# Laying out the backward step's results by SBUF-to-SBUF transfers in place of TensorE transposes in three blocks of four (S4 convolution with a gated FFN, one Trainium2 core)

## The chip, the core and the metric

The kernel runs on one core of one Trainium2 chip. The metric is the device time of one execution in microseconds (us). A core has TensorE (PE; its weight loads are listed apart as PEld), VectorE (DVE), ScalarE (ACT), GpSimd (POOL) and SyncE (SP), which here only issues DMA transfers. Transfers can be issued from SyncE's, ScalarE's and GpSimd's queues. Each engine works through its own instructions in order; semaphores tie the engines together.

## The reference

```python
x  = A_u                                    # (1, 2048, 512)
xn = layernorm(x)
s  = A_ref(xn, ...)                         # S4 convolution along the 2048 steps
g  = silu(gelu(xn @ w1 + b1) @ w2 + b2)     # F = 1792
return x + s * g

# A_ref, for each of D = 512 channels, N = 128 states:
P = exp((dt * A)[:, :, None] * arange(L))   # complex
K = einsum("dn,dnl,dn->dl", C, P, dt * B).real
y = irfft(rfft(u, 2L) * rfft(K, 2L))[:L] + u * Dskip
```

All arrays are float32. The change lies in the convolution: the product of two spectra and the way back from it.

## The kernel before

The first part (until about 404 us of the span) computes the layer norm, the feed-forward network and the 512 convolution kernels. Its order is written out by hand in `ORDER`, token by token. It ends with the gate `g` in DRAM (`gd`) and the kernels in DRAM (`kgd`). The change doesn't touch it.

The second part does the convolution in `NB = 4` blocks of 128 channels. The transform of 2048 points is split as 32 x 64. For each block `b` there are eight steps `g`, and `slot(b, g)` (L1020) writes down what each step issues. `tc.manual_schedule()` keeps that order on every engine. The functions, in the order of a step:

- `second_dft(b, g)` (L874): 64 small matmuls into a PSUM tile "ri" of two buffers; L883 in the profile.
- `last_dft(b - 1, t)` (L969, matmuls L975) of the block before: the last, 32-point transform of the way back. It reads `yy[b, q4, "s"]` and the table `gc`, and writes two banks. In blocks 1 and 2 it runs in steps 5 and 7; for block 2, within block 3, in step 4 and at the very end.
- `last_out` (L978) multiplies its result with the gate on VectorE (L982, into `gb`) and adds `x` on GpSimd (L983, into `xb`); `store` (L985) sends `xb` out by eight transfers on SyncE's queue (L992).
- `first_dft(b + 1, ...)` (L856, matmuls L864) in even steps: the first transform of the next block; `first_out` (L867) copies it to `X` on ScalarE (L870).
- `back_dft(b, j, h)` (L914, matmuls L918) in odd steps, for the group `j` whose products were made two steps earlier; four matmuls for each half `h`, each 128x128. Step 1 does group 3 of the block before.
- `spectrum` (L887) copies half of the spectrum to `uh` on ScalarE (L891).
- `back_out(b, j, h)` (L921) copies the result of `back_dft` from PSUM into the tile `Z` on ScalarE (L930).
- `product` (L896) on VectorE (L900), and in odd steps `combine` (L902), four instructions on VectorE (L912, L910) that make the tile `Y`, the operand of `back_dft`.
- `swings(b - 1, q4)` (L997): `swing` (L932) turns four 128x128 pieces of `Z` by TensorE transposes (L936), `swing_out` (L939) copies them from PSUM to an SBUF tile "bs" (L944). For blocks 0 and 1 these run in steps 3 and 5 of the next block, two `q4` in each; for block 2 in steps 2 to 5 of block 3, one in each; for block 3 at the end.
- `tail_load` (L949): loads `gb` (from `gd`, L961 or L955) and `xb` (from the input, L964 or L957) for the later `last_out`. A tail is six transfers on SyncE's queue. The tiles have three buffers, so the load of the fourth tail of a block (step 5) follows the stores of step 5 in the queue. In block 3, GpSimd's queue carries the tails of block 3 (steps 1 to 4) beside SyncE's for block 2 (steps 0 to 3).
- `side_load`, `side_turn`, `kernel_load`, `side_skip`: inputs for the block after the next one, in steps 3, 6 and 7 of blocks 0 and 1.

PSUM tiles from `bank` (L804) go round over four banks in turn. After the 32 steps, the rest of block 3 is written out by hand (L1125 to L1144).

In the profiled execution the second part starts at 405.9 us. Block 1 starts (its first `second_dft`) at 436.5, block 2 at 473.1, block 3 at 509.6.

Of the kernel before, what the change touches and what calls it, by code (L numbers as in the profile page):

```python
# [11 lines left out]
F32 = mybir.dt.float32  # L12
# [8 lines left out]
P = 128  # L21
# [4 lines left out]
N1, N2 = 32, 64  # L26
NB = 4
# [25 lines left out]
G.4 S.1.3 W.6 S.2.0 WS.4.3.1 S.2.1 R.3 A.0.0 H.4 KL.1.0 LC.3 TF.2.0 S.2.2 S.2.3 TH.2.0 B.0.0 WS.5.0  # L53
TF.3.0 WS.5.1 C.0.0 TH.3.0 WB.6 BB TL.2.0 A.0.1 WS.5.2 KL.0.1 Z.0 S.3.0 TL.3.0 B.0.1 TF.3.1 TH.3.1 C.0.1
TL.3.1 WS.5.3.1 P.1 LD.2 P.0 LD.3 WS.6.0 S.3.1 WS.6.1 S.3.2 S.3.3 A.1.0 LS.5.1 TF.2.1 N.0.0 TH.2.1 F.5.0
LS.4.1 B.1.0.1 F.5.1 KL.1.1 WS.6.2 TL.2.1 N.0.1 G.5 C.1.0 R.4 F.6.0 LK.0 S.4.0 S.4.1 A.1.1 KL.2.0 F.6.1
B.1.1 LR.4 E.0.0 H.5 F.7.0 G.6 Z.1 F.7.1 WS.6.3 C.1.1 H.6 A.2.0 F.8.0 S.4.2 E.0.1 E.0.2 KL.2.1 R.5 N.1.0
N.1.1 B.2.0.1 Q.0 R.6 G.7 Z.2 LC.4 C.2.0 E.1.0 E.1.1 KL.3.0 F.8.1 S.4.3 U.0 H.7 S.5.0 G.8 S.5.1 A.2.1
B.2.1 KL.3.1 P.1 LD.4 F.9.0 C.2.1 TF.4.0 KL.4.0 UD.0 R.7 LC.5 F.9.1 E.1.2 S.5.2 P.1 N.2.0 G.9 TH.4.0
S.5.3 A.3.0 TF.4.1 LL.6 S.6.0 Q.1 S.6.1 H.8 B.3.0.1 C.3.0 S.6.2 S.6.3 TL.4.0 A.3.1 KL.4.1 N.2.1 O.0.0 U.1  # L60
B.3.1 LD.5 O.0.2 O.0.1 E.2.0 F.10.0 P.1 Z.3 TH.4.1 UD.1 C.3.1 S.7.0 S.7.1 KL.5.0 N.3.0 E.2.1 TL.4.1
F.10.1 E.2.2 N.3.1 P.1 O.0.3 S.7.2 A.4.0 R.8 E.3.0 B.4.0.1 H.9 F.11.0 S.7.3 G.10 C.4.0 S.8.0 LS.6.0 Q.2
# [68 lines left out]
def _shape_constants():  # L131
    n1 = np.arange(N1)[:, None]
    k1 = np.arange(N1)[None, :]
    a = 2 * np.pi * n1 * (k1 + 0.25) / N1
    cf = np.tile(np.stack([np.cos(a), -np.sin(a)], 1), (G, 1, 1))
    cg = np.zeros((2, N1, 2, 3, N1))
    for hh in range(2):
        for c, v in enumerate((np.cos(a).T, -np.sin(a).T)):
            cg[hh, :, c, 0] = v
            cg[hh, :, c, 1:].reshape(N1, N1, 2)[:, :, hh] = v  # L140
    cg = cg.reshape(P, 3 * N1)
    n2 = np.arange(N2)[:, None]
    k2 = np.arange(N2)[None, :]
    cm = np.zeros((2, N2, N1, 3, N2))
    ct = np.zeros((2, N2, N1, 2, N2))
    for k in range(N1):
        th = 2 * np.pi * (n2 * (k + 0.25) / L + n2 * k2 / N2)
        c, s = np.cos(th), np.sin(th)
        cm[:, :, k, 0, :] = c
        cm[:, :, k, 1, :] = s  # L150
        cm[:, :, k, 2, :] = -s
        ct[0, :, k, 0, :] = c.T / L
        ct[1, :, k, 0, :] = -s.T / L
        ct[0, :, k, 1, :] = s.T / L
        ct[1, :, k, 1, :] = c.T / L
    ct = ct.reshape(P, N1, 2, 2, 2, 16).transpose(0, 1, 4, 5, 3, 2)
    cb = np.zeros((CH, NPC, CH, NPH))
    for d in range(CH):
        cb[d, :3, d, :N1] = N2 * np.arange(N1)
        cb[d, :3, d, N1:] = np.arange(N2 // 2) + 0.5  # L160
        cb[d, 3:, d, :N1] = 1.0
    f = np.float32
    return {
        "cf": cf.reshape(P, 2 * N1).astype(f),
        "cg": cg.astype(f),
        "cm": cm.reshape(P, N1 * 3 * N2).astype(f),
        "ct": ct.reshape(P, N1 * P).astype(f),
        "cb": cb.reshape(CH * NPC, CH * NPH).astype(ml_dtypes.bfloat16),
    }
# [3 lines left out]
def kernel(  # L173
# [5 lines left out]
    V, A, GP, PE, SY = nc.vector, nc.scalar, nc.gpsimd, nc.tensor, nc.sync  # L179
# [121 lines left out]
    SB = {}  # L301
# [4 lines left out]
    sg = ExitStack()  # L306
# [544 lines left out]
    def side_skip(b):  # L851
        for h in range(2):
            k0 = side[b][1][h][:, :, 0]
            GP.tensor_add(k0, k0, dsk[:, b, h * DB // 2:(h + 1) * DB // 2])
# [17 lines left out]
    sp, sm, yy = {}, {}, {}  # L872
# [41 lines left out]
    def back_dft(b, j, h):  # L914
        Y = yy[b, j].rearrange("p j a m -> p (j a) m")
        p = bank(f"sa{b}_{j}_{h}")
        for e in range(4):
            PE.matmul(p[:, e, :], Y[:, 4 * h + e, :], SB["tcn"][:, 8 * j + 4 * h + e, :], start=True, stop=True)  # L918
        yy[b, j, h] = p

    def back_out(b, j, h, engs=(A,)):  # L921
        if (b, "Z") not in yy:
            yy[b, "Z"] = SB["pm"].tile([P, 32, 2, N1, 2], F32, tag="Z", name=f"Z{b}", bufs=2)
        k = 8 * j + 4 * h
        src = yy.pop((b, j, h)).rearrange("p k (x h c) -> p x h k c", h=2, c=2)
        dst = yy[b, "Z"][:, :, :, k:k + 4, :]
        w = 4 // len(engs)
        for i, eng in enumerate(engs):
            n = slice(w * i, w * i + w)
            eng.copy(dst[:, :, :, n], src[:, :, :, n]) if eng is A else eng.tensor_copy(dst[:, :, :, n], src[:, :, :, n])  # L930

    def swing(b, q4, jj, wide=None):  # L932
        Z = yy[b, "Z"].rearrange("p (j r t q) h k c -> p j r t q (h k c)", j=2, r=2, t=2)
        p = bank(f"w{b}_{q4}_{jj}") if wide is None else wide[:, jj]
        for e in range(4):
            PE.transpose(p[:, e, :], Z[:, jj, q4 // 2, q4 % 2, e, :], ident)  # L936
        yy[b, q4, jj] = p
# [28 lines left out]
    def new_tail(b, q4):  # L966
        return tuple(SB["pm"].tile([P, 4, P], F32, tag=m, name=f"{m}{b}_{q4}", bufs=3) for m in ("gb", "xb"))
# [29 lines left out]
    def swings(b, q4, wide=None, engs=(A, A)):  # L997
        for jj in range(2):
            swing(b, q4, jj, wide)
            if wide is None:  # L1000
                swing_out(b, q4, jj, engs[jj])
        if wide is not None:
            for jj in range(2):
                swing_out(b, q4, jj, engs[jj])
# [15 lines left out]
    def slot(b, g):  # L1020
        nxt = b + 1 < NB
        i = g // 2
        sa = (b, i - 1) if i else (b - 1, 3)
        if sa[0] < 0 or g % 2 == 0:
            sa = None
        last = b == NB - 1
        sw = {2: (0,), 3: (1,), 4: (2,), 5: (3,)} if last else {3: (0, 1), 5: (2, 3)}
        ls = {4: (0,)} if last else {5: (0,), 7: (1,)}
        second_dft(b, g)
        if b:  # L1030
            for q4 in ls.get(g, ()):
                last_dft(b - 1, q4)
                if not last:
                    last_out(b - 1, q4, (GP, GP))
                    store(b - 1, q4)
        if nxt and g % 2 == 0:
            first_dft(b + 1, i // 2, i % 2, range(G))
        if sa:
            back_dft(*sa, 0)
            back_dft(*sa, 1)  # L1040
        spectrum(b, g)
        if nxt and g % 2 == 0:
            first_out(b + 1, i // 2, i % 2)
        if sa:
            back_out(*sa, 0)
            back_out(*sa, 1)
        product(b, g)
        if (b, g) == (0, 0):
            gx[0, 0, "t"] = new_tail(0, 0)
        if g % 2 and (b, g) != (NB - 1, 7):  # L1050
            combine(b, i, 1, V)
        if b == NB - 1 and g > 5:
            js = slice(2 * g - 12, 2 * g - 10)
            combine(b, 3, 1, V, js)
            combine(b, 3, 0, V, js)
        elif g % 2:
            combine(b, i, 0, V)
        if last:
            for q4 in ls.get(g, ()):
                last_out(b - 1, q4, (GP, GP))  # L1060
                store(b - 1, q4)
        if b:
            for q4 in sw.get(g, ()):
                swings(b - 1, q4)
        if last and g == 0:
            big = SB["pf"].tile([P, 2, N1, P], F32, tag="X0", name="last")
            for q4 in range(4):
                gx[b, q4, "t"] = (big[:, 0, 4 * q4:4 * q4 + 4], big[:, 1, 4 * q4:4 * q4 + 4])
        if last and g == 2:
            spare = SB["pf"].tile([P, 4, 4, P], F32, tag="in", name="spare", bufs=2)  # L1070
            for i in range(2):
                gx[b - 1, 2 + i, "t"] = (spare[:, 2 * i], spare[:, 2 * i + 1])
        when = (0, 1, 2, 3) if last else (0, 1, 2, 5)
        if b and g in when:
            tail_load(b - 1, when.index(g))
        if last and 0 < g < 5:
            tail_load(b, g - 1, GP, g > 2)
        if last and g == 0:
            SY.dma_start(gc2, cg[:, N1:])
        if b + 2 < NB and g == 3:  # L1080
            side_load(b + 2)
        if b + 2 < NB and g == 6:
            side_turn(b + 2)
            kernel_load(b + 2)
        if b + 2 < NB and g == 7:
            side_skip(b + 2)

    with tc.manual_schedule():
        prologue()
# [5 lines left out]
    with tc.manual_schedule():  # L1095
# [9 lines left out]
        for p in "S0 F00 S1 S2 F01 S3 L0 F10 L1 A0 F11 A1 L2 L3 A2 A3".split():  # L1105
            if p[0] == "F":
                k = int(p[1]), int(p[2])
# [17 lines left out]
        b = NB - 1  # L1125
# [49 lines left out]
```

## Time and profile before

| | |
|---|---|
| median of 3 runs | 559.72 us (559.51 to 559.85) |
| profiled execution | 559.77 us, its span 558.0 us |
| granted TensorE clock, mean | 0.998 |
| instructions | 17143 |
| DMA traffic | 86.92 MB in 108345 packets |
| busy in 418 to 434 us (block 0), of 16.0 | PE 16.00, DVE 12.14, ACT 9.13, POOL 1.04 |
| busy in 480 to 498 us (block 2), of 18.0 | PE 18.00, DVE 10.97, ACT 10.84, POOL 0.00 |
| busy in 514 to 528 us (block 3), of 14.0 | PE 13.66, DVE 12.30, ACT 6.40, POOL 6.46 |

How to read the lines of the profile. In a timeline a line is: start (us from the span's start), length (us), engine, line of the kernel, operation, written tile <- read tiles, shapes, how many in a row (x), and in square brackets how long the engine stood idle before it and what it then waited for. Lines of one kind that follow one another are merged, so the length of "x16" is that of all sixteen together; matmuls overlap, so the distance to the next line's start says what they cost. "SPq", "ACTq" and "POOLq" are the issuing of transfers; the transfer itself goes on afterwards. In a group line the fields are: line, engine, operation, tiles, shapes, count | busy us, mean ns of one | idle us before. A line of DMA issues gives written tile <- read tensor, queue, count, KB each, and the median time from issue to landing.

### The profile page before, as it was taken

To read this page: it belongs to the slowest core of one execution; us is meant where nothing else is said; L and a number is where in the kernel's file an instruction comes from. 1 tells how busy PE (TensorE), PEld (TensorE's weight loads), DVE (VectorE), ACT (ScalarE), POOL (GpSimd) and SP (SyncE) were. 2 spreads that over 40 slices of the span, in tenths; PEclk is the share of its full clock that TensorE was granted. 3 is DMA by queue.
4 is the path that set the end of the run, shared out by engine and by line. 5 is a ranking of instruction groups with operands and counts; after the bars stand their busy time and mean duration, and the time that the engine had idled before them with its cause. 6 is when DMAs were issued, how large, how long until landed. Compare 5 with 4: busy or idle time off the path is not lost.

```text
span 558.0 us, 17143 instructions
## 1 busy us (share of the span) xinstructions
PE 540.2 (97%) x7179; PEld 432.1 (77%) x7179; DVE 454.2 (81%) x697; ACT 407.8 (73%) x602; POOL 296.3 (53%) x403
## 2 busy tenths in 40 slices
PE   8899999999999999999999999999999999999995
PEld 7567777777777777767777777777889998988872
DVE  6899999999997799988988969877357657767874
ACT  3589997977598999668989798995355565564542
POOL 5639585776966769857718747540320305014323
PEclk9999999999999999999999999999999999999999
DMA  8959337267468392426167049205965583615945
GB/s 188 288 161 311 84 96 210 61 210 228 135 189 269 133 295 81 143 75 192 57 188 219 21 114 186 61 11 181 365 245 79 140 128 95 191 46 127 197 120 113
DMA packets 108345, 86.92 MB, mean 156 GB/s; under 512 B 44294, under 2 KB 87562, under 8 KB 108268
## 3 DMA queue, kind: packets, MB, share of 16 engines
q1 hardware_dynamic: 97584, 65.37, 43.8%
q0 software_dynamic: 9568, 19.93, 12.1%
q8 instruction: 56, 0.92, 0.7%
q10 hardware_dynamic: 1116, 0.53, 0.4%
q14 instruction: 21, 0.17, 0.1%
HBM read 52.25 MB, written 33.55 MB: 154 GB/s over the span
## 4 chain that ended last, share of the span: by engine, by line
PE 68%; DVE 16%; issue 6%; DMA 5%; SPq 2%; ACT 1%; POOL 1%; DVEq 0%; POOLq 0%
PE z L295 8%; PE z L296 7%; PE z L297 7%; PE f L256 7%; PE f L258 7%; PE f L257 7%; PE s L883 6%; PE kg L656 5%; PE s L864 4%; PE sa L918 3%; DMA w2s<-in_B_w_dram 2%; PE ph L595 2%; PE w L936 2%; DVE e L641 2%; DVE hl L282 2%
## 5 line engine op out<-in xcount | busy, mean ns | idle before, releaser
L618 POOL TENSOR_TENSOR mm<-mm,rc 128x32 f32<-128x32 f32 (+4 forms) x150 | 110.7, 738 | 11.8
L295 PE MATMUL z<-w2h,hh 128*128 128x512 f32 x224 | 97.9, 437 | 0.0
L256 PE MATMUL f<-xh,w1h 128*128 128x512 f32 x220 | 92.0, 418 | 0.5 <-ACT hf L270 0.5
L297 PE MATMUL z<-w2h,hl 128*128 128x512 f32 x224 | 88.5, 395 | 0.9 <-DVE hl L282 0.9
L296 PE MATMUL z<-w2l,hh 128*128 128x512 f32 x224 | 88.7, 396 | 0.0
L258 PE MATMUL f<-xh,w1l 128*128 128x512 f32 x220 | 86.9, 395 | 1.5 <-DVE w1l L241 1.5
L257 PE MATMUL f<-xl,w1h 128*128 128x512 f32 x220 | 86.7, 394 | 0.0
L883 PE MATMUL s<-X,mc 64*64 64x128 f32 x2048 | 63.5, 272 | 0.9 <-issue 0.9
L900 DVE TENSOR_TENSOR t<-s,uh 128x512 f32<-128x512 f32 x64 | 41.1, 685 | 25.9 <-ACT uh L891 25.6
L883 PEld LDWEIGHTS s<-X,mc 64*64 64x64 f32 x2048 | 56.0, 133 | 4.8 <-issue 2.7
L641 DVE TENSOR_TENSOR e<-mm,ra 128x1024 f32<-128x1024 f32 x32 | 47.8, 1495 | 4.7 <-POOL mm L618 3.2
L297 PEld LDWEIGHTS z<-w2h,hl 128*128 128x128 f32 x224 | 42.1, 188 | 11.7 <-DVE hl L282 1.8
L258 PEld LDWEIGHTS f<-xh,w1l 128*128 128x128 f32 x220 | 41.3, 188 | 11.9 <-DVE w1l L241 2.1
L615 POOL COPY mm<-rc 128x32 f32<-128x32 f32 x30 | 15.4, 512 | 65.4 <-DVE e L648 49.0
L256 PEld LDWEIGHTS f<-xh,w1h 128*128 128x128 f32 x220 | 41.5, 189 | 10.3 <-ACT hf L270 1.2
L282 DVE TENSOR_TENSOR hl<-hf,hh 128x512 fp32r<-128x512 f32 x56 | 46.7, 838 | 3.4 <-ACT hh L276 3.3
L295 PEld LDWEIGHTS z<-w2h,hh 128*128 128x128 f32 x224 | 42.5, 190 | 9.0
L609 DVE SCALAR_TENSOR_TENSOR ra<-ra,ph 128x512 f32<-128x512 f32 x64 | 43.6, 681 | 6.9 <-ACT ra L603 6.0
L296 PEld LDWEIGHTS z<-w2l,hh 128*128 128x128 f32 x224 | 42.3, 189 | 7.9
L257 PEld LDWEIGHTS f<-xl,w1h 128*128 128x128 f32 x220 | 41.4, 188 | 8.9
L870 ACT COPY X<-s 128x512 f32<-128x512 f32 x56 | 28.9, 598 | 25.6 <-PE s L864 25.6
L645 DVE TENSOR_TENSOR e<-mm,ra 128x1024 f32<-128x1024 f32 x32 | 45.6, 1425 | 0.0
(185 smaller groups left out, 1146.2 us busy)
## 6 DMA issues: line engine op xcount, KB each, us to landing
x<-in_A_u_dram SPq DMA_DIRECT2D x16, 256.0 KB
xs<-x SPq DMA_DIRECT2D x16, 256.0 KB
xt_h<-xh POOLq DMA_DIRECT2D x4, 1024.0 KB, 5.4
xt_l<-xl POOLq DMA_DIRECT2D x4, 1024.0 KB, 7.3
kgd<-ko SPq DMA_DIRECT2D x32, 128.0 KB
za<-zo SPq DMA_DIRECT2D x4, 1024.0 KB
xh<-xt_h POOLq DMA_DIRECT2D x4, 1024.0 KB, 6.8
xl<-xt_l POOLq DMA_DIRECT2D x4, 1024.0 KB, 10.1
```

The costliest lines, as they stand in the source:

```text
L256: PE.matmul(p, wh[:, k, :], xh[:, k, :], start=(k == 0), stop=False)
L257: PE.matmul(p, wh[:, k, :], xl[:, k, :], start=False, stop=False)
L258: PE.matmul(p, wl[:, k, :], xh[:, k, :], start=False, stop=(k == KD - 1))
L282: V.tensor_sub(hl, hf, hh)
L295: PE.matmul(z, hh[:, s], wh, start=(f0 == 0 and not rows), stop=False)
L296: PE.matmul(z, hh[:, s], wl, start=False, stop=False)
L297: PE.matmul(z, hl[:, s], wh, start=False, stop=(f0 == FA - 1))
L609: V.scalar_tensor_tensor(ra[:, 0, c], ra[:, 1, c], MAGIC, p, op0=ALU.subtract, op1=ALU.subtract)
L618: GP.tensor_mul(mv[:, :, 0:3:2, w:2 * w], mv[:, :, 0:3:2, 0:w], rc[:, 2 + 2 * i:4 + 2 * i, :].rearrange("p j c -> p c j").unsqueeze(3).to_ ...
L641: V.tensor_mul(e1, m1.unsqueeze(1).to_broadcast([P, 2, CH, N1]), ra[:, :, :, :N1])
L645: V.tensor_mul(e2[:, :, :, :H], m2[:, :, :H].unsqueeze(1).to_broadcast([P, 2, CH, H]), ra[:, :, :, dn])
L883: PE.matmul(p[ka * 64:(ka + 1) * 64, r, o, :, jj], mc[h, k, ((0, 2), (1, 0))[c][o], :], xf[b][h, c, :, k, :], start=(c == 0), stop=(c == 1 ...
```

## The change

In blocks 0, 1 and 2 the transposes are left out. `back_dft` swaps its two operands there, so that its result already has the channels along the row (`p` holds, for each `k`, 128 positions by 128 channels). `spread_out` copies that from PSUM to an SBUF tile `v` on ScalarE, in place of `back_out`. `spread` then issues four transfers from SBUF to SBUF. Each takes one `k`: 128 partitions with 512 bytes each go to four partitions of the tile `S` (`8 j + k`, and 32, 64 and 96 further), 16 KB to each. There are eight spreads to a block, one at the end of a step, alternately from ScalarE's queue (odd steps) and GpSimd's (even steps), from step 3 of the block to step 2 of the next: 96 transfers in all, 64 KB each. After the last of them `S` is taken as the operand of `last_dft`. Block 3 goes on as before, with the order of rows in `Z` and in the tables `cg` and `ct` changed to fit both forms.

```diff
-    cg = np.zeros((2, N1, 2, 3, N1))
+    cg = np.zeros((2, 2, N1, 3, N1))
     for hh in range(2):
         for c, v in enumerate((np.cos(a).T, -np.sin(a).T)):
-            cg[hh, :, c, 0] = v
-            cg[hh, :, c, 1:].reshape(N1, N1, 2)[:, :, hh] = v
+            cg[hh, c, :, 0] = v
+            cg[hh, c, :, 1:].reshape(N1, N1, 2)[:, :, hh] = v
...
-    ct = ct.reshape(P, N1, 2, 2, 2, 16).transpose(0, 1, 4, 5, 3, 2)
+    ct = ct.reshape(P, N1, 2, 2, 2, 16).transpose(0, 1, 3, 2, 4, 5)
...
         for e in range(4):
-            PE.matmul(p[:, e, :], Y[:, 4 * h + e, :], SB["tcn"][:, 8 * j + 4 * h + e, :], start=True, stop=True)
+            w, m = SB["tcn"][:, 8 * j + 4 * h + e, :], Y[:, 4 * h + e, :]
+            PE.matmul(p[:, e, :], *((w, m) if b < NB - 1 else (m, w)), start=True, stop=True)
         yy[b, j, h] = p
+
+    def spread_out(b, j, h):
+        if h == 0:
+            yy[b, j, "v"] = SB["pm"].tile([P, 8, P], F32, tag="bs", name=f"v{b}_{j}", bufs=3)
+        dst = yy[b, j, "v"][:, 4 * h:4 * h + 4].rearrange("p k (x r) -> p k r x", r=2)
+        A.copy(dst, yy.pop((b, j, h)).rearrange("p k (r x) -> p k r x", r=2))
+
+    def spread(b, j, h, q):
+        v = yy[b, j, "v"]
+        if (b, "S") not in yy:
+            yy[b, "S"] = SB["pm"].tile([P, 32, P], F32, tag="Z", name=f"S{b}", bufs=2)
+        for k in range(4 * h, 4 * h + 4):
+            q.dma_start(yy[b, "S"][8 * j + k::N1].rearrange("a x d -> a (x d)"), v[:, k])
+        if j == 3 and h == 1:
+            t = yy.pop((b, "S")).rearrange("p (j r t q) d -> p j r t q d", j=2, r=2, t=2)
+            for q4 in range(4):
+                yy[b, q4, "s"] = t[:, :, q4 // 2, q4 % 2]
 
     def back_out(b, j, h, engs=(A,)):
         if (b, "Z") not in yy:
-            yy[b, "Z"] = SB["pm"].tile([P, 32, 2, N1, 2], F32, tag="Z", name=f"Z{b}", bufs=2)
+            yy[b, "Z"] = SB["pm"].tile([P, 32, 2, 2, N1], F32, tag="Z", name=f"Z{b}", bufs=2)
         k = 8 * j + 4 * h
-        src = yy.pop((b, j, h)).rearrange("p k (x h c) -> p x h k c", h=2, c=2)
-        dst = yy[b, "Z"][:, :, :, k:k + 4, :]
+        src = yy.pop((b, j, h)).rearrange("p k (h c x) -> p (h c) x k", h=2, c=2)
+        dst = yy[b, "Z"][:, :, :, :, k:k + 4].rearrange("p x h c k -> p (h c) x k")
...
-        sw = {2: (0,), 3: (1,), 4: (2,), 5: (3,)} if last else {3: (0, 1), 5: (2, 3)}
...
         if sa:
-            back_out(*sa, 0)
-            back_out(*sa, 1)
+            for h in range(2):
+                (back_out if last and i else spread_out)(*sa, h)
...
-        if b:
-            for q4 in sw.get(g, ()):
-                swings(b - 1, q4)
...
         if b + 2 < NB and g == 7:
             side_skip(b + 2)
+        if (b or g > 2) and (not last or g < 3):
+            sb, sg = (b, g - 3) if g > 2 else (b - 1, g + 5)
+            spread(sb, sg // 2, sg % 2, (A, GP)[sg % 2])
```

More of the change, by code (lines that the diff above doesn't have):

```diff
@@ L932, in swing @@
     def swing(b, q4, jj, wide=None):
-        Z = yy[b, "Z"].rearrange("p (j r t q) h k c -> p j r t q (h k c)", j=2, r=2, t=2)
+        Z = yy[b, "Z"].rearrange("p (j r t q) h c k -> p j r t q (h c k)", j=2, r=2, t=2)
         p = bank(f"w{b}_{q4}_{jj}") if wide is None else wide[:, jj]
```

## The prediction

> **What bounds the kernel now.** I read the page first (busy shares, then the chain of work that ended last), then TensorE's timeline over the last stage, then those of VectorE, GpSimd, ScalarE and SyncE's queue at each place where TensorE stood still.
>
> ```profile
> span 558.0 us, 17143 instructions
> PE 540.2 (97%) x7179; PEld 432.1 (77%) x7179; DVE 454.2 (81%) x697; ACT 407.8 (73%) x602; POOL 296.3 (53%) x403
> PE 68%; DVE 16%; issue 6%; DMA 5%; SPq 2%; ACT 1%; POOL 1%; DVEq 0%; POOLq 0%
> ```
>
> TensorE is busy 97% of the span and holds most of the chain. So whatever is taken off TensorE is worth its length wherever TensorE is the last to arrive, and nothing where it waits anyway. The timeline of TensorE (start, length, engine, line) says where that is:
>
> ```profile
> 452.03 1.91 PE L936 MATMUL w<-ident,Z 128*128 128x128 f32 x16
> 453.87 1.98 PE L883 MATMUL s<-X,mc 64*64 64x128 f32 x64
> ...
> 478.89 2.05 PE L918 MATMUL sa<-tcn,Y 128*128 128x128 f32 x16
> ...
> 496.12 1.09 PE L975 MATMUL y<-bs,gc 64*32 64x512 f32 x16
> 497.14 2.05 PE L918 MATMUL sa<-tcn,Y 128*128 128x128 f32 x16
> 499.03 1.91 PE L936 MATMUL w<-ident,Z 128*128 128x128 f32 x16
> ...
> 514.17 0.46 PE L918 MATMUL sa<-tcn,Y 128*128 128x128 f32 x2 [0.82 <-DVE Y L910]
> 514.80 1.83 PE L918 MATMUL sa<-tcn,Y 128*128 128x128 f32 x14 [0.17 <-DVE Y L910]
> ...
> 526.16 1.09 PE L975 MATMUL y<-bs,gc 64*32 64x512 f32 x16
> 527.18 1.09 PE L936 MATMUL w<-ident,Z 128*128 128x128 f32 x8
> 528.20 1.98 PE L883 MATMUL s<-X,mc 64*64 64x128 f32 x64
> ```
>
> From 452 to 514 TensorE never stands still; then `back_dft` of block 2's last group waits 0.82 and 0.17 us for VectorE. Why VectorE is late there is read from its own timeline and from SyncE's queue:
>
> ```profile
> 476.39 1.40 DVE L910 TENSOR_TENSOR Y<-t,t 64x512 f32<-64x512 f32 x2
> ...
> 509.20 0.69 DVE L982 TENSOR_TENSOR gb<-y,gb 128x512 f32<-128x512 f32 x1 [0.65 <-DMA gb<-gd]
> ```
>
> ```profile
> 499.43 4.04 SPq L992 DMA_DIRECT2D out_dram<-xb  x8
> 503.56 0.45 SPq L961 DMA_DIRECT2D gb<-gd  x1
> 504.12 1.80 SPq L964 DMA_DIRECT2D xb<-in_A_u_dram  x2
> 505.98 0.45 SPq L961 DMA_DIRECT2D gb<-gd  x1
> 506.48 1.06 SPq L964 DMA_DIRECT2D xb<-in_A_u_dram  x2
> ```
>
> This is a **second chain**. `last_dft` (496.12) lets GpSimd add; SyncE then stores eight pieces and only behind them loads the next tail, whose buffers the stores free. The tail's second `gb` lands at 509.2, VectorE multiplies, then makes `Y`, and TensorE gets it. From `last_dft` on this chain has a length of its own: fewer transposes don't shorten it.
>
> **The change part by part.** *Removed from TensorE:* the `swing` transposes of blocks 0 to 2.
>
> ```profile
> L936 PE MATMUL w<-ident,Z 128*128 128x128 f32 x96 | 11.9, 274 | 0.0
> ```
>
> By starts, sixteen cost 453.87 - 452.03 = 1.84 us, eight cost 528.20 - 527.18 = 1.02 us or a little less. What each is worth:
>
> - Block 1, step 3: TensorE-bound, 1.84 gained.
> - Block 1, step 5: `Y` is ready at 476.39 + 1.40 = 477.79, TensorE takes it at 478.89, a slack of 1.1. So 1.1 of 1.84 is gained.
> - Block 2, step 3: 1.84 gained.
> - Block 2, step 5 (499.03): lies inside the second chain, for which TensorE already waits. Nothing gained.
>
> Together 4.8 us off by the time `back_dft` runs at 514.
>
> *Last block.* Here the new transfers take the place of the transposes on the path. `last_dft(2, 0)` (526.16) now needs all 32 transfers of block 2, and the last four are issued by GpSimd in step 2, behind twelve tail loads; four more stand ahead of those loads. GpSimd's timeline and the landing times of that stretch:
>
> ```profile
> 510.81 1.27 POOL L983 TENSOR_TENSOR xb<-gb,xb 128x512 f32<-128x512 f32 x1 [0.91 <-DMA xb<-in_A_u_dram]
> 512.02 0.55 POOL L961 DMA_DIRECT2D last<-gd  x1
> 512.57 1.15 POOL L964 DMA_DIRECT2D last<-in_A_u_dram  x2
> ...
> 517.53 1.11 POOL L964 DMA_DIRECT2D last<-in_A_u_dram  x2
> 519.53 0.57 POOL L955 DMA_DIRECT2D last<-gd  x1 [0.89 <-DMA last<-in_A_u_dram]
> 520.25 0.63 POOL L957 DMA_DIRECT2D last<-in_A_u_dram  x1
> 521.20 0.62 POOL L957 DMA_DIRECT2D last<-in_A_u_dram  x1 [0.32 <-DMA last<-gd]
> ```
>
> ```profile
> last<-gd POOLq DMA_DIRECT2D x4, 128.0 KB, 4.3
> last<-in_A_u_dram POOLq DMA_DIRECT2D x8, 64.0 KB, 5.2
> last<-gd POOLq DMA_DIRECT2D x2, 256.0 KB, 5.8
> last<-in_A_u_dram POOLq DMA_DIRECT2D x4, 128.0 KB, 6.9
> ```
>
> Twelve loads take from 512.02 to 518.64. A spread is 64 KB in 512-byte rows, like one L964, so eight of them add 8 x 0.55 = 4.4: 523.0. GpSimd's queue has eight completion semaphores, which the program hands out in turn; the waits of 0.89 and 0.32 show the thirteenth transfer and a later one held until earlier ones had landed, so I add 1.2: 524.2. With a landing of 5.2 (same size) that is 529.4, against 526.16: 3.3 us late. Behind it two steps of eight transposes are gone (those at 527.18 and at 532.00), which gives back 1.8; the two ahead of it only lengthen the wait. Net +1.5. Bounds: 4.3 and 6.9 for the landing. I take 6.9, since the stretch is full and the last four come after everything else in the queue: +1.7 more. Sum so far: -4.8 + 1.5 + 1.7 = -1.6.
>
> *SyncE's burst.* SyncE and ScalarE share eight further semaphores. That a transfer waits for an unrelated one is in the waits of SyncE's queue:
>
> ```profile
> SPq L964 <- DMA gb<-gd: 1.9, 2, 1.4
> SPq L992 <- DMA in<-kgd: 0.9, 1, 0.9
> ```
>
> In step 5 of blocks 1 and 2 ScalarE issues four transfers just when SyncE issues the fourteen of the second chain. The fourteen took 507.54 - 499.43 = 8.1 us, 0.58 each. Four more in the same ring cost 4 x 0.58 = 2.3 at most, and nothing if the ring is never full. A pair of L964 took 1.80 there where 1.06 is usual, so it is nearly full already: I take 1.5 for each of the two bursts, 3.0 in all. Behind SyncE's delay stand `gb`, VectorE's product and `Y`, and so TensorE.
>
> *ScalarE.* For each group, two `back_out` and the `swing_out` copies become two `spread_out` of the same form, and four issues follow in every second step.
>
> ```profile
> 421.17 0.59 ACT L930 COPY Z<-sa 128x512 f32<-128x512 f32 x1 [0.31 <-PE sa L918]
> 423.15 0.59 ACT L891 COPY uh<-s 128x512 f32<-128x512 f32 x1 [1.40 <-PE s L883]
> ...
> 551.47 0.88 ACTq L992 DMA_DIRECT2D out_dram<-last  x2
> ```
>
> ```profile
> 427.62 1.29 DVE L900 TENSOR_TENSOR t<-s,uh 128x512 f32<-128x512 f32 x2 [2.29 <-ACT uh L891]
> ```
>
> Four issues at 0.44 fill 421.76 to 423.5, 0.4 us past the start of the next `uh`, which is queued behind them; VectorE waits for `uh`, but has 2.29 us idle before its next product, and that hides it. Cost 0. Without the cover it is 0.4 in each of twelve steps, 4.8 us; below zero there is nothing to win, as ScalarE bounds no stretch.
>
> *Moved at no cost:* the swapped operands of `back_dft` (both 128x128), the reordered tables, block 3's `back_out` (same element count). The landing of blocks 0 and 1 has several microseconds: their last spreads are issued in step 2 and read in step 5.
>
> The sum is -1.6 + 3.0 = **+1.4 us**. The profiled execution took 559.77, of which 1.77 lie outside the span, and 0.05 over the median shown; so 559.77 + 1.4 = **561.2**.
>
> **A rule against the change.** A transfer's rate here is read from a stretch with SyncE's tail loads alone, 482 to 492:
>
> ```profile
> q1 hardware_dynamic: 1809, 1.25, 44.6%
> ```
>
> That is 0.446 x 16 x 10 us / 1809 = 39 ns of one DMA engine for a packet; 128 packets over sixteen engines are 0.3 us, over four engines 1.3 us. The Trainium skill, "DMA: Bandwidth & Descriptors" (Why a DMA increments its semaphore by 16 and not by 1), says that a transfer runs on the largest number of engines up to sixteen that divides the outermost counts of both sides: 128 and 4 here, so four. "SBUF — State Buffer" (Door 1) adds that partitions 32 apart share a port, which puts the four transfers of one step on two ports of sixteen. By these the first rival below holds; no row of this profile shows such a transfer.
>
> **The rivals.** *Narrow transfers.* Each spread writes only four partitions. If that confines it to four engines, the four of a step take 4 x 1.3 = 5.0 us instead of 1.3. The last ones of block 2 land 3.8 later, and the semaphores that ScalarE's four hold come back late: SyncE, which goes round the eight in about 4 us, would wait some 3 us per burst instead of 1.5, +3.0 for both. 1.4 + 3.8 + 3.0 = +8.2: **568.0**. For it: a destination of 16 KB on each of four partitions. Against: the 39 ns come from rows that are read from HBM, and here both sides are in SBUF, which may be quicker.
>
> *The transfers hide.* If they land in 4.3 us and the eight shared semaphores never run out, the bursts cost nothing: -4.8 + 1.5 - 0.9 = -4.2: **555.6**, faster. It decides as soon as the second `gb` lands within 9.7 us of the first store, as now (509.2 - 499.43), and block 2's last spread by about 528. For it: TensorE's eight blocks of transposes are surely gone. Against: the 1.80 us pair and GpSimd's 0.89.
>
> *ScalarE becomes the bound:* the issues wait 1 us each, the uncovered 0.4 grows towards 4 in a step, and `uh`, then `X`, hold TensorE: with 1 us lost in each of twelve steps, some 573. Against it: SyncE is quiet during most of block 0.
>
> **How the numbers follow.** The forecast has a chance of 0.47 (558 to 564.5), the hidden transfers 0.33 (553 to 559), narrow transfers 0.15, ScalarE 0.05. The range reaches down to 555.0 and up to 567.5; that leaves out about 0.08 below and 0.11 above. A change of 0.2%, 1.1 us, is about what can be told from none. Faster, below 558.6, gets most of the second case and a little of the first: 0.33. Within it lie some 0.15, mostly of the first case, and slower has 0.52.
>
> **What would show it.** In the new profile no L936 of blocks 0 to 2; the `back_dft` at the turn to block 3 waits about 4 us for `Y` (0.99 now); `last_dft(2, 0)` waits for a DMA into `S`, and TensorE's idle time there is over 4 us; SyncE's fourteen transfers of step 5 take over 9 us; ScalarE's spread issues take 0.5 us each where SyncE rests. If `last_dft(2, 0)` doesn't wait, the last-block term is wrong and the change is faster. If TensorE already stands still in block 0, ScalarE's cover was misjudged, and it is far slower.

## The result, and the profile after

The changed kernel takes **646.3 us** (644.8 to 648.5), against 559.6 for the kernel before on the same chip: a ratio of 1.1534, 95% interval 1.1505 to 1.1562. It is 86.7 us slower, where 561.2 was forecast and 568.0 was the price of the rival with narrow transfers. Times here and below are medians of the executions in the chip's fast state. Five lines of the page of the changed kernel: the span, the busy shares, the clock that TensorE was granted in forty slices, and the chain of waits by engine and by line.

```profile
span 646.0 us, 17106 instructions
PE 553.3 (86%) x7083; PEld 439.7 (68%) x7083; DVE 454.8 (70%) x697; ACT 394.5 (61%) x578; POOL 327.6 (51%) x451
PEclk9999999999999999999999999997589675888689
PE 51%; DVE 17%; DMA 17%; SPq 6%; issue 4%; POOL 2%; ACT 0%; ACTq 0%; DVEq 0%; POOLq 0%
DMA S<-v 7%; PE z L295 7%; PE z L296 6%; PE z L297 6%; PE f L256 6%; PE f L258 6%; PE f L257 6%; PE kg L656 4%; DMA xb<-in_A_u_dram 4%; DMA out_dram<-xb 4%; SPq L819 3%; PE s L883 3%; PE s L864 3%; PE ph L595 2%; DVE hl L282 2%
```

TensorE has 96 matmuls fewer and is yet busy for longer; its clock falls from the 28th slice on, at 436 us, soon after the first transfers into `S` (422.77 below), and transfers, which held 5% of the chain, now hold 17%. The stage itself, in one stretch from 405 us to the end (length, busy time and count of TensorE, of its weight loads, of VectorE, ScalarE and GpSimd, granted clock, share of the DMA engines, GB/s), before and after:

```profile
405.00:558.00 153.00, 143.43 (x3329) 125.10 (x3327) 103.83 (x156) 79.85 (x146) 40.15 (x46) 0.99 0.58 134
```

```profile
405.00:646.00 241.00, 157.12 (x3240) 133.47 (x3236) 103.03 (x157) 67.49 (x123) 73.01 (x94) 0.83 0.74 113
```

88.0 us longer: TensorE's busy time grew by 13.7, though it has fewer matmuls to do, and the other 74.3 are standing still. Beside e3 below, which has the same matmuls, the busy time is 22.2 longer (157.12 against 134.90, at a clock of 0.83 against 0.98). Who waited for whom in that stretch of the changed kernel (total, times, longest):

```profile
DVE t L900 <- ACT uh L891: 98.0, 22, 15.9
ACT uh L891 <- DMA S<-v: 63.7, 6, 17.9
PE sa L919 <- ACT X L870: 28.0, 3, 13.9
PE y L993 <- ACT X L870: 14.2, 3, 8.6
ACT uh L891 <- DMA gb<-gd: 16.3, 1, 16.3
...
ACT uh L891 <- DMA xb<-in_A_u_dram: 14.5, 1, 14.5
ACT uh L891 <- DMA out_dram<-xb: 11.0, 2, 6.8
```

This reads as a chain. TensorE waits for `X` and VectorE for `uh`, both made by ScalarE, and ScalarE waits ahead of `uh` for the landing of transfers, its own and SyncE's: 105.5 us in ten waits, each put down to the landing that came last, and with the issuing itself, some 2 us, in each. Its timeline from step 3 of block 0 on:

```profile
422.77 2.65 ACTq L933 DMA_DIRECT2D S<-v  x4
...
430.69 8.14 ACTq L933 DMA_DIRECT2D S<-v  x4
438.92 0.58 ACT L891 COPY uh<-s 128x512 f32<-128x512 f32 x1 [7.66 <-DMA S<-v]
...
455.13 6.20 ACTq L933 DMA_DIRECT2D S<-v  x4
461.43 0.58 ACT L891 COPY uh<-s 128x512 f32<-128x512 f32 x1 [16.27 <-DMA gb<-gd]
```

The first four issues take 2.65 us, the next four 8.14, with `uh` queued behind them. At 461.43 ScalarE had stood for 16.27 us, and what it waited for last was the landing of a `gb`, a tail that it neither loads nor reads: the two queues share eight semaphores in one turn, and a transfer waits for whoever held its semaphore last. By that turn it is the `gb` that SyncE issued at 448.38, so it took some 12 us to land. That issue, and two lines of SyncE's own waits in the stretch, which show the other direction:

```profile
448.38 0.45 SPq L979 DMA_DIRECT2D gb<-gd  x1
```

```profile
SPq L982 <- DMA S<-v: 16.0, 6, 5.1
...
SPq L979 <- DMA S<-v: 7.7, 3, 3.9
```

SyncE's tail loads stand for 23.7 us in nine waits for transfers into `S`. Each queue hands its lateness to the other. TensorE then runs dry and comes back at a lower clock (16 `back_dft` matmuls took 2.05 us before):

```profile
462.55 3.79 PE L919 MATMUL sa<-Y,tcn 128*128 128x128 f32 x16 [12.32 <-ACT X L870]
```

Two more views say what a transfer is. The DMA queues of before and of after (ScalarE's transfers are in q10; packets, MB, time as a share of 16 engines' span), and the landing of GpSimd's transfers:

```profile
q10 hardware_dynamic: 1116, 0.53, 0.4%
```

```profile
q10 hardware_dynamic: 7452, 3.68, 3.8%
...
S<-v POOLq DMA_DIRECT2D x48, 64.0 KB, 9.1
```

ScalarE's 48 transfers made 7452 - 1116 = 6336 packets, 132 each: 128 rows and four others, one for each of four engines, as the experiments bear out (in the trace the four are of 4 bytes, and the semaphore's last four counts come one by one). Their engine time is 0.038 x 16 x 646.0 - 0.004 x 16 x 558.0 = 357 us, 7.4 us a transfer and 56 ns a packet. Spread over four engines that is 1.9 us. The four of a step, if they go one after another, need 7.4 us; a step of the stage before took 4.1:

```profile
L883 PE MATMUL s<-X,mc x2048: 266/269/321, 405.9 to 536.4; 64*64 64x128 f32 x187
```

(32 groups of 64 in 130.5 us). 24 steps of 7.4 instead of 4.1 would be 79 us more. That this estimate lies close to the 86.7 shows nothing by itself: only twelve of the steps are ScalarE's, and GpSimd's 48 transfers took longer, (0.162 x 16 x 646.0 - 0.121 x 16 x 558.0) / 48 = 12.4 us each by the queue q0 of the two pages. Nor is engine time a transfer's own price alone. Packets of several queues can overlap on an engine (the share is 1.22 between 420 and 430 us), and then each one's time has waiting in it: SyncE's 97584 packets, the same before and after, took 43.8% of 558.0 us and then 42.3% of 646.0, 460 us of engine time more.

### The profile page after: what moved, and what is told of

It reads as the page before. It is cut to its first block, busy times and chain, and to the rows that moved or that the text cites. A ratio compares the mean times of both kernels' runs of the same rounds, so it can differ in the third digit from the quotient of the medians.

```text
span 646.0 us, 17106 instructions
## 1 busy us (share of the span) xinstructions
PE 553.3 (86%) x7083; PEld 439.7 (68%) x7083; DVE 454.8 (70%) x697; ACT 394.5 (61%) x578; POOL 327.6 (51%) x451
## 3 DMA queue, kind: packets, MB, share of 16 engines
q1 hardware_dynamic: 97584, 65.37, 42.3%
q10 hardware_dynamic: 7452, 3.68, 3.8%
## 4 chain that ended last, share of the span: by engine, by line
PE 51%; DVE 17%; DMA 17%; SPq 6%; issue 4%; POOL 2%; ACT 0%; ACTq 0%; DVEq 0%; POOLq 0%
DMA S<-v 7%; PE z L295 7%; PE z L296 6%; PE z L297 6%; PE f L256 6%; PE f L258 6%; PE f L257 6%; PE kg L656 4%; DMA xb<-in_A_u_dram 4%; DMA out_dram<-xb 4%; SPq L819 3%; PE s L883 3%; PE s L864 3%; PE ph L595 2%; DVE hl L282 2%
## 5 line engine op out<-in xcount | busy, mean ns | idle before, releaser
L891 ACT COPY uh<-s 128x512 f32<-128x512 f32 x32 | 19.1, 599 | 135.9 <-DMA S<-v 63.7
L257 PE MATMUL f<-xl,w1h 128*128 128x512 f32 x220 | 86.7, 394 | 0.0
L883 PE MATMUL s<-X,mc 64*64 64x128 f32 x2048 | 71.8, 293 | 17.3 <-ACT Z L948 11.6
L883 PEld LDWEIGHTS s<-X,mc 64*64 64x64 f32 x2048 | 63.4, 146 | 23.5 <-ACT Z L948 11.8
L933 POOL DMA_DIRECT2D S<-v x48 | 32.8, 688 | 58.3 <-ACT v L926 56.5
L919 PE MATMUL sa<-Y,tcn 128*128 128x128 f32 x192 | 32.4, 336 | 28.3 <-ACT X L870 28.0
L919 PEld LDWEIGHTS sa<-Y,tcn 128*128 128x128 f32 x192 | 29.6, 243 | 35.3 <-ACT X L870 30.0
L641 DVE TENSOR_TENSOR e<-mm,ra 128x1024 f32<-128x1024 f32 x32 | 47.8, 1494 | 4.4 <-POOL mm L618 3.2
```

Of the source, the lines that this page charges most:

```text
L257: PE.matmul(p, wh[:, k, :], xl[:, k, :], start=False, stop=False)
L641: V.tensor_mul(e1, m1.unsqueeze(1).to_broadcast([P, 2, CH, N1]), ra[:, :, :, :N1])
L883: PE.matmul(p[ka * 64:(ka + 1) * 64, r, o, :, jj], mc[h, k, ((0, 2), (1, 0))[c][o], :], xf[b][h, c, :, k, :], start=(c == 0), stop=(c == 1 ...
L919: PE.matmul(p[:, e, :], *((w, m) if b < NB - 1 else (m, w)), start=True, stop=True)
```

## The experiments

| Kernel | us | ratio to before, 95% interval |
|---|---|---|
| changed kernel | 646.3 | 1.1534 (1.1505 to 1.1562) |
| e1: transfers onto all 128 partitions | 583.5 | 1.0401 (1.0349 to 1.0454) |
| e2: all 96 issued by GpSimd | 658.3 | 1.1734 (1.1671 to 1.1797) |
| e3: no transfers | 554.7 | 0.9900 (0.9872 to 0.9927) |
| e4: all 96 issued by SyncE | 666.1 | 1.1872 (1.1799 to 1.1946) |
| e5: four partitions, 4 apart | 610.0 | 1.0869 (1.0819 to 1.0919) |
| e6: 16 neighbouring partitions | 592.9 | 1.0565 (1.0491 to 1.0640) |
| e7: 128 partitions, all by GpSimd | 565.8 | 1.0086 (1.0056 to 1.0116) |
| e8: two blocks by way of DRAM | 594.3 | 1.0576 (1.0523 to 1.0630) |
| e9: as changed, products don't wait | 631.3 | 1.1276 (1.1209 to 1.1343) |
| e10: as e2, products don't wait | 641.4 | 1.1453 (1.1385 to 1.1521) |

Each ratio is to the kernel before as it ran beside that kernel, at 559.6 to 561.0 us. Two theories stood first. *Narrow*: the transfers are slow since each writes few partitions, and everything else follows. *Ring*: issuing is the trouble, since ScalarE sits in SyncE's turn of semaphores and must wait in order.

**e1, 128 partitions.** The same 64 KB, one row to each partition, from the same queues.

```
-            q.dma_start(yy[b, "S"][8 * j + k::N1].rearrange("a x d -> a (x d)"), v[:, k])
+            q.dma_start(yy[b, "S"][:, 8 * j + k], v[:, k])
```

> The changed kernel with the same 96 transfers from the same queues, of the same 64 KB in 512-byte rows, but each from 128 partitions straight to 128 partitions of S instead of to four (S then holds its rows in another order, so the way back is computed from wrongly laid out rows). Narrow theory (a transfer with four destination partitions is slow, so the eight shared semaphores come back late and hold ScalarE): 553 to 562 us. Ring theory (any 48 further transfers in ScalarE's queue hold it, however quick they are): 630 to 646 us.

583.5: between the two ranges, so each theory holds a part. ScalarE's waits of e1, its queue and GpSimd's landing:

```profile
ACT uh L891 <- DMA S<-v: 43.8, 8, 11.5
```

```profile
q10 hardware_dynamic: 8028, 3.68, 2.8%
...
S<-v POOLq DMA_DIRECT2D x48, 64.0 KB, 4.4
```

Packets are now 144 a transfer, sixteen engines, and the landing is 4.4 us in place of 9.1. 62.8 of the 86.7 us go with the destination alone. ScalarE still waits 43.8 us for semaphores.

**e2 and e4, another queue.** The narrow transfers, all issued by GpSimd (which has eight semaphores of its own), or all by SyncE.

```
-            spread(sb, sg // 2, sg % 2, (A, GP)[sg % 2])
+            spread(sb, sg // 2, sg % 2, GP)    # e4: SY
```

> The changed kernel with all 96 transfers issued by GpSimd, to four partitions each as in the change; ScalarE issues none. If ScalarE held by its issues is what costs the time: TensorE runs freely in block 0, and the end comes at 555 to 580 us, set by GpSimd's own eight semaphores. If slow transfers cost it wherever they are issued: GpSimd is held instead, last_dft waits for S, 600 us or more.

> The changed kernel with all 96 transfers in SyncE's queue, to four partitions each. Narrow theory: SyncE is held by its own semaphores, its loads and stores come late, and the end is 620 us or more, though ScalarE is free in block 0. If only ScalarE's in-order blocking matters: 560 to 575.

658.3 and 666.1. Taking ScalarE out of the ring cures nothing while the transfers stay narrow, so the ring alone fell as an explanation. The largest of TensorE's waits in e2 has a name that stood for 2.5 us in the changed kernel, and the landing is longer still:

```profile
PE s L864 <- issue: 25.9, 4, 9.4
```

```profile
S<-v POOLq DMA_DIRECT2D x96, 64.0 KB, 11.3
```

"issue" is time for which the profile shows no releaser; e10 comes back to it.

**e3, no transfers.** `S` is zeroed by GpSimd once a block instead.

```
+            GP.memset(yy[b, "S"], 0.0)
...
-            q.dma_start(yy[b, "S"][8 * j + k::N1].rearrange("a x d -> a (x d)"), v[:, k])
+            pass
```

> The changed kernel without the 96 transfers; GpSimd fills S with zeros once a block instead, so the way back of blocks 0 to 2 is computed from zeros. It shows what the removed transposes are worth alone. By the prediction's sum 4.8 us are gained up to the turn to block 3, and up to 3.6 more in block 3 where nothing waits for S: 551 to 555 us. If the second chain through SyncE's stores takes all of it: 557 to 559.5.

554.7, that is 5.9 us under the 560.5 of before beside it. This is all that the removed transposes are worth, and the second chain is why it isn't more. In e3, VectorE and TensorE at the turn to block 3, and the place at which both kernels have that turn behind them, in e3 and before:

```profile
506.16 0.69 DVE L1001 TENSOR_TENSOR gb<-y,gb 128x512 f32<-128x512 f32 x1 [4.06 <-DMA gb<-gd]
```

```profile
508.19 3.12 PE L883 MATMUL s<-X,mc 64*64 64x128 f32 x64 [3.04 <-DVE t L900]
...
513.83 3.72 PE L883 MATMUL s<-X,mc 64*64 64x128 f32 x128
```

```profile
516.56 1.98 PE L883 MATMUL s<-X,mc 64*64 64x128 f32 x64
```

VectorE waits for the second `gb`, and TensorE for VectorE. Block 3 starts 6.5 us earlier than before (503.17 against 509.63), but behind this wait 2.7 are left (513.83 against 516.56), and the span ends 5.2 earlier: the other 2.5 come in block 3.

**e5 and e6, where the rows land.** Four partitions 4 apart instead of 32 apart, still 132 packets; and sixteen neighbours, eight rows each, 144 packets.

```
+            p0 = 16 * (2 * j + k // 4) + k % 4
+            q.dma_start(yy[b, "S"][p0:p0 + 13:4].rearrange("a x d -> a (x d)"), v[:, k])
...
+            p0, x0 = 16 * (2 * j + k // 4), 8 * (k % 4)
+            q.dma_start(yy[b, "S"][p0:p0 + 16, x0:x0 + 8], v[:, k])
```

> The changed kernel with each transfer still to four partitions, but four apart instead of 32 apart (S holds its rows in another order, so the way back is computed from wrongly laid out rows). If the number of engines that carry one transfer (four) sets its length: as the change, 635 to 655 us. If it is where the four partitions lie: 590 to 620 us.

> The changed kernel with each transfer to sixteen neighbouring partitions, eight rows of 512 bytes each (again rows in another order). If the number of engines sets the length: near the run with 128 destination partitions, 580 to 592 us. If it is how few partitions are written at a time: 605 to 640 us.

ScalarE's queue in e5 and in e6:

```profile
q10 hardware_dynamic: 7452, 3.68, 2.9%
```

```profile
q10 hardware_dynamic: 8028, 3.68, 3.5%
```

e5, 610.0: with the number of engines unchanged, the place of the four partitions is worth 36.3 us. A packet takes 0.029 x 16 x 608.2 less the 36 of before, over 6336, 39 ns instead of 56. e6, 592.9, at the edge of the engines' range, takes another 17.1, and e1 another 9.4. So both things count, and in this order the place counts more. The 17.1 go with four times the engines and four times the partitions at once; no run changed one without the other. And time per packet doesn't rank the runs: e6's is 42 ns, (0.035 x 16 x 588.4 - 36) / 6912, more than e5's. The Trainium skill, "DMA: Bandwidth & Descriptors" (Why a DMA increments its semaphore by 16 and not by 1), gives four engines for four partitions and sixteen for the other two, which the packets bear out; "SBUF — State Buffer" (Door 1) has partitions 32 apart on one port, and the 36.3 us agree with it in kind, though no view here shows a port.

**e7, 128 partitions by GpSimd.** Both edits, of e1 and of e2.

> The run with 128 destination partitions, with all 96 transfers in GpSimd's queue. If what is left there (583.5 against 554.7 us without transfers) comes from ScalarE waiting in the ring of eight semaphores that it shares with SyncE: 553 to 562 us. If it comes from the transfers themselves or from GpSimd being late: 575 to 590.

565.8: 17.8 less than e1. That is what ScalarE's part in the issuing costs when transfers are quick, with its waits in the ring, net of what the further issues cost GpSimd. The transfers themselves are no cheaper from the other queue: 4.7 us of engine time each in e1's q10 (224 over 48) and 4.5 in e7's q0, (0.168 x 16 x 564.0 - 0.121 x 16 x 558.0) / 96. What is left against e3 is 11.1 us. In e7's timeline of VectorE its tail products wait for GpSimd, whose additions now stand behind its issues, and for `gb`:

```profile
477.42 0.69 DVE L1000 TENSOR_TENSOR gb<-y,gb 128x512 f32<-128x512 f32 x1 [5.89 <-POOL xb L1001]
...
515.04 0.69 DVE L1000 TENSOR_TENSOR gb<-y,gb 128x512 f32<-128x512 f32 x1 [3.50 <-DMA gb<-gd]
```

**e8, by way of DRAM.** Blocks 0 and 1 send 512 KB a group to DRAM and fetch `S` from there in pieces of 256 KB, 24 transfers in place of 64; block 2 keeps its transposes.

```
+        GP.dma_start(vd[b][8 * j:8 * j + 8].rearrange("k p d -> p k d"), yy.pop((b, j, "v")))
...
+            GP.dma_start(yy[b, "S"][32 * a + 16 * u:32 * a + 16 * u + 16], vd[b][n, 32 * a:32 * a + 32])
```

> Another way to the same layout, with the reference's result: for blocks 0 and 1 GpSimd sends each v to DRAM in one transfer of 512 KB and fetches S from there in transfers of 256 KB to sixteen partitions; block 2 goes by TensorE transposes as before the change. ScalarE issues nothing. By the prediction's terms 3 to 5 us of transposes are gained: 554 to 557 us, faster than before; if the way through DRAM makes last_dft or the second chain wait: 559 to 566.

594.3, a miss on both sides. GpSimd's timeline shows the round trip, and SyncE's queue what it does to others:

```profile
463.84 1.93 POOL L937 DMA_DIRECT2D S<-vd  x4 [13.88 <-DMA vd<-v]
```

```profile
454.69 23.77 SPq L820 DMA_DIRECT2D raw<-xs  x4
```

GpSimd is held for 13.88 us until its own writes have landed, and four `raw` loads that SyncE issued in 6.15 us before take 23.77.

**e9 and e10, nobody waits for the data.** The transfers of the changed kernel and of e2, but `last_dft` of blocks 0 to 2 reads a small zeroed tile.

```
+            yy["R"] = SB["pm"].tile([P, 1, 4, P], F32, name="R").to_broadcast([P, 2, 4, P])
+            GP.memset(yy["R"][:, 0], 0.0)
...
-                yy[b, q4, "s"] = t[:, :, q4 // 2, q4 % 2]
+                yy[b, q4, "s"] = yy["R"]
```

> All 96 transfers as in the changed kernel (same queues, same four partitions), but `last_dft` of blocks 0 to 2 reads a small zeroed tile instead of what they wrote, so no product waits for a landing. If the 86.7 us come from results that land too late for `last_dft`, the time falls to 555 to 580. If they come from ScalarE and SyncE holding each other up in issuing, and from slow transfers in the way of other ones, almost nothing changes: 625 to 650, with ScalarE still waiting for completions ahead of `uh`.

> The same with all 96 transfers issued by GpSimd; ScalarE and SyncE then wait for none of them. What is left is GpSimd's own holding (its additions stand behind the transfers), the three buffers that the transfers read from, and the traffic itself. If late landings made the 658.3 us of that arrangement, 555 to 580; if GpSimd's holding and the traffic do, 625 to 660, with VectorE's `gb` waiting for GpSimd and TensorE's waits for no visible releaser kept.

631.3 and 641.4: late results cost 15 and 17 us; the bulk stays when nobody waits for them. In e9 ScalarE is held as before (73.8 us for transfers into `S` alone, 63.7 in the changed kernel). e10 is the telling one, for there TensorE never waits for a transfer and ScalarE once, for 0.8 us. The stretch from 405 us in e3 and in e10, and TensorE's waits in e10:

```profile
405.00:553.00 148.00, 134.90 (x3232) 116.43 (x3230) 103.30 (x156) 68.22 (x122) 51.16 (x49) 0.98 0.61 138
```

```profile
405.00:640.00 235.00, 168.73 (x3236) 142.58 (x3235) 106.14 (x157) 69.46 (x123) 106.29 (x143) 0.79 1.03 115
```

```profile
PE s L883 <- issue: 31.6, 10, 8.9
PE s L864 <- issue: 20.9, 3, 9.4
PE sa L919 <- issue: 2.4, 1, 2.4
```

87.0 us longer than e3: 33.8 are TensorE at 0.79 of its clock, and 52.9 are "issue" (54.9, against 2.0 in e3). The DMA engines' share is 1.03, full; but full engines alone don't do it, for the kernel before had 1.01 between 514 and 528 us and no such stall there. TensorE's timeline, and the queue of instructions in the half microsecond from 437.0, say what it lacks:

```profile
432.06 0.89 PE L864 MATMUL s<-fc,in 32*128 32x64 f32 x22
441.22 2.82 PE L864 MATMUL s<-fc,in 32*128 32x64 f32 x42 [8.27 <-issue]
...
457.94 1.75 PE L883 MATMUL s<-X,mc 64*64 64x128 f32 x52
463.97 1.12 PE L883 MATMUL s<-X,mc 64*64 64x128 f32 x12 [4.28 <-issue]
```

```profile
q8 instruction: 1, 0.02, 27.4%
```

The same queue over the whole of e10:

```profile
q8 instruction: 55, 0.90, 0.7%
```

It stops in the middle of a group of 64, where its data is plainly there. Between the two breaks lie 42 + 64 + 16 + 64 + 64 + 64 + 16 + 52 = 382 matmuls, twice that in instructions with their weight loads. That queue moves packets of 16 KB (0.90 MB in 55). Between 430 and 441 us it began one, after 437.0, which took 0.274 x 16 x 0.5 = 2.2 us, and TensorE resumed about 2 us after its end; the packet begun after 460.5 precedes its resumption at 463.97 in the same way. The trace has eleven "issue" stalls of over 2 us in this stretch; every one ends 1.6 to 4.0 us after the end of such a packet, eight of them 1.6 to 2.1 after it. So the instructions themselves come over the clogged DMA engines. That the fetch ends these stalls is read from this order; no run moved it by itself.

## Why the prediction was wrong

**Right in kind, with luck in the number: the transposes.** -4.8 was forecast for them up to the `back_dft` at the turn to block 3, and -5.9 measured for the whole of e3. The two aren't the same stretch: up to that turn e3 gains 2.7. The second chain was named rightly, and its 4.06 us wait stands where `gb` was said to hold the path; it takes back more than was counted, and block 3 gives the rest. Of the signs that were set, no L936 of blocks 0 to 2 is left, and SyncE's burst of fourteen takes over 9 us; `back_dft` at the turn to block 3 waits 0.17 us for `Y` in the changed kernel, behind 2.27 of the products before it for VectorE, and not 4.

**Wrong: "ScalarE. ... Cost 0".** This is the step that failed. It priced four issues at 0.44 each, took it that they don't wait, and covered their 0.4 us of overhang with VectorE's 2.29 of idle time. The 0.44 came from two stores at the very end, when nothing else was under way. Here four took 2.29 to 12.04 us, and `uh` was held for 105.5 us in all. The prediction named this as a rival, ScalarE as the bound, and priced it by a 1 us hold in each step, 573; it spoke against it that SyncE is quiet during block 0. But the hold needs no burst from SyncE: slow transfers keep the semaphores for longer than a step (the `gb` above for 12 us), whoever issued them. And ScalarE isn't the whole of it: in e2 it issues nothing, and the time is 658.3. The last test that it set, that TensorE standing still early means far slower, came true.

**Wrong beneath it: "so 64 KB in 512-byte rows, like one L964".** A spread was given the cost of a load of the same size. It has the size, and another destination. The first rival had four engines and, from a row, 39 ns a packet, 5.0 us for a step's four; measured, 56 ns and 7.4 us. That was the right mechanism, short by a third. What was missed is the comparison beside it: a step lasts 4.1 us. If the spreads of successive steps go over the same few engines, which no view shows, then even at 5.0 us they can't keep up, every one starts later than the last, and the queues behind them fill. Instead, the 5.0 was counted once as a later landing (+3.8) and twice as a burst (+3.0).

**Undersized: SyncE's bursts.** 1.5 us each was forecast. From SyncE's queue in the changed kernel, the fourteen transfers of block 1's and of block 2's step 5, first and last:

```profile
498.27 8.60 SPq L1010 DMA_DIRECT2D out_dram<-xb  x8
...
509.51 1.06 SPq L982 DMA_DIRECT2D xb<-in_A_u_dram  x2
...
560.35 10.88 SPq L1010 DMA_DIRECT2D out_dram<-xb  x8
...
573.42 1.06 SPq L982 DMA_DIRECT2D xb<-in_A_u_dram  x2
```

12.3 and 14.1 us, against 8.1: 4.2 and 6.0 more.

**Undersized: the last block.** `last_dft(2, 0)` was forecast to be 3.3 us late, 5.0 with the longer landing, of which 1.5 + 1.7 went into the sum. It waits 10.2 us:

```profile
PE y L993 <- DMA spare<-in_A_u_dram: 10.2, 1, 10.2
```

The view names a tail load into `spare`, which `last_dft` doesn't read. In the trace's semaphore events TensorE goes through those of the three queues one after another, and the last one that it waits for, until 613.63, is that of ScalarE's last transfer into `S`, issued at 597.17, 16.4 us earlier. So the wait for `S` came, as was said, but through ScalarE's transfers; the forecast looked for it in GpSimd's.

**What the 86.7 us consist of.** Going from the changed kernel to e5, e6, e1, e7 and e3 takes off 36.3, 17.1, 9.4, 17.8 and 11.1 us: the place of the partitions, four engines and partitions against sixteen of each, 16 partitions against 128, ScalarE's part in the issuing, and what is left of the transfers with GpSimd's issues. These are 91.7, from which the gain of 5.9 goes (and 0.9 by which the kernel before was slower beside e3). The order matters, and several steps rest on kernels that ran twice (e6 at 590.1 and 595.7), so the small ones are rough. With narrow transfers, moving them out of the ring (e2) gains nothing, since the fetch of instructions and GpSimd's own queue suffer in its place. No arrangement tried beats the kernel before; e3, which moves nothing, has only 5.9 us to give.

## What to carry to other kernels

Before a transfer takes the place of compute, set the engine time of one step's transfers against the length of the step: if it doesn't fit, expect not a later landing but a queue that grows, and reaches everything that shares engines, semaphores or an issuing engine with it. That is how the runs here are read, and no run varied it alone; e1 fits its step by far (four transfers of 4.7 us over sixteen engines, 1.2 us) and is still 23 us slower than the kernel before. Size alone doesn't give that time: how many partitions the destination has, and how far apart they lie, made 62.8 us of difference with the same bytes. An engine in order that issues transfers waits with all its work for whichever transfer had the semaphore last, here SyncE's as well as its own, so an issue is free only as long as nothing is slow.

## What was not expected of the hardware

- Four destination partitions 32 apart cost 56 ns of engine time a packet from ScalarE's queue, waiting included, four that lie 4 apart 39 ns, sixteen neighbours 42, and 128 partitions 0.028 x 16 x 581.2 less 36, over 48 x 144, 32 ns, all for 512-byte rows within SBUF.
- Slow transfers starve TensorE of instructions, by the order of events in e10: 54.9 us of its time there, 2.7 in e7 with the same bytes from the same queue. In the changed kernel itself such stalls are 5.9 us. The Trainium skill, "Runtime: NRT & Kernel Launch" (Instruction fetch mechanics), says that each engine's sequencer fetches blocks of 256 instructions by a DMA queue of its own while it executes the block before, at a cost that is mostly hidden. The packets of 16 KB agree, and by that figure the 764 instructions between the two breaks are, as an estimate, some three blocks. In e10 the stall was up to 9.4 us at a time, and not hidden.
- TensorE's stalls count twice: after them its clock is lower (0.79 over the stage in e10), and the same work takes 33.8 us longer than in e3.
